# A sparse-attention and two-MLP kernel: weights loaded and converted in tiles of 512 columns with buffers of their own

## The chip, the cores and the metric

The kernel runs on one core of a Trainium2 chip. The metric is device time in microseconds (us), the median of several executions. TensorE does the matmuls, VectorE (DVE) and ScalarE (ACT) the elementwise work, SyncE (SP) issues the loads and stores.

## The reference

Attention with 4 batches, 8 heads, 576 positions and head size 64 is followed by two MLPs on 2304 tokens (512 to 2048 to 512). Half of the heads see the last 32 positions, the other half every 32nd position. All of it is float32, and the weights reach the kernel as float64.

```
scores = where(mask, scale * q @ k.T, -1e9);  attn = softmax(scores);  x = attn @ v
h = x @ w_in;   x = (s * relu(h)**2 + b) @ w_out          # first MLP
h = x @ w_in2;  out = (h * cos(h)) @ w_out2               # second MLP
```

## The kernel before

**Number format.** Every matmul of the MLPs is done three times on numbers that are split in a high and a low part: high x high, high x low, low x high. A weight tile is 128 x 512 numbers; `w` holds its high part and its low part. A weight arrives as a float64, so as two 32-bit words, and has to be put together as a float32 first. `convert_ops` does that on VectorE with four bit operations (L128 a multiplication, L129 a shift, L131 and L136 each a two-operand operation), into a tile `wtmp`. `split_hi` (L109, on ScalarE) then writes the high part and `split_lo` (L112, on VectorE) the low part.

**Where raw weights stand.** The pool `st` has four buffers of 2 KB a partition. A tile is loaded in two halves of 256 columns (`w_job`, L193 and L194, two `wraw`), and `wtmp` takes a third buffer of the same four. So a tile needs three of the four buffers, and the second half of the next tile waits for the first half of this one. The first four tiles, (0,0), (1,0), (0,1) and (1,1), are loaded whole at the start into space of the weights themselves (`w_early_load`, L155, `wearly`), and each of their operations has 512 columns. Key (n, k) is chunk n of the hidden dimension (0 to 15 first MLP, 16 to 31 second) and k the matrix (0 in, 1 out). 64 tiles are converted, 60 of them through `wraw`.

**Order.** The program is written as one sequence. MLP work goes in slots: 2 MLPs x 4 passes x 5 token blocks x 4 chunks = 160 slots. A slot has four groups of matmuls for `h` (`mm_h`, L521) and, for the slot two before it, four groups into the accumulators (`mm_2`, L575 and L578). After each group the program takes a step of attention (while there is any), of the elementwise stages, and of the background list `bg`: `bg_step(n)` adds n to a counter and issues one operation of a conversion for each whole one in it. n is BG0 = 1.5 in the first four slots, BG = 0.6 after that, and EARLY_BG = 0.6 for each step before them, when attention's first batch runs. `weight(n, k)` issues what is left of a conversion at once when a matmul needs it. In each pass of 20 slots the seven entries of `W_AT`, and one more line at its start, put the conversions of eight tiles on the list. A scheduling layer then moves instructions: on each engine they stand in the order that it chose.

**Attention around it.** A step of attention's softmax on VectorE is a maximum (L318), a scaling (L319), and, after ScalarE's exponentials, a sum step (L356), a reciprocal (L357) and the normalisation (L358), which TensorE's transposes (L366) wait for. The second MLP's elementwise chain ends with a multiplication on VectorE (L552) that reads `h_ps` and so frees its PSUM bank for the matmuls two slots later.

**Loads.** All DMAs are issued by SyncE, in its order: attention's `qk`, `v`, `rq`, `rs`, `rv`, then `wraw`, at the end `out`.

Of the kernel before, what the change touches and what calls it, by code (L numbers as in the profile page):

```python
# [8 lines left out]
F32 = mybir.dt.float32  # L9
F32R = mybir.dt.float32r  # L10
BF16 = mybir.dt.bfloat16
U32 = mybir.dt.uint32
AF = mybir.ActivationFunctionType
ALU = mybir.AluOpType
# [5 lines left out]
P = 128  # L20
NC = DM // P
NF = DFF // P
# [17 lines left out]
NWB = (7, 6)  # L40
W_AT = {3: (0, 0), 6: (0, 1), 9: (1, 0), 12: (1, 1), 15: (2, 0), 18: (3, 0), 19: (2, 1)}
W_AT0 = {8: (0, 0), 10: (0, 1), 12: (1, 0), 14: (1, 1), 15: (2, 0), 18: (3, 0), 19: (2, 1)}
BG = 0.6
BG0 = 1.5
RATE = [1.0, 0.6]
EARLY_BG = 0.6
ALAG = 3
NPB = 6
FIRST = [
# [32 lines left out]
def net(ctx, tc, qk, vloc, vstr, w1, w2, s, b, out):  # L82
    nc = tc.nc
    w_raw = [w1.bitcast(U32), w2.bitcast(U32)]
# [4 lines left out]
    st_p = ctx.enter_context(tc.tile_pool(name="st", bufs=4))  # L89
# [18 lines left out]
    def split_hi(dst_hi, src):  # L108
        nc.scalar.activation(dst_hi, src, AF.Copy)  # L109

    def split_lo(dst_lo, src, hi):
        nc.vector.tensor_tensor(dst_lo, src, hi.bitcast(F32), ALU.subtract)  # L112


    wtile, ready = {}, set()

    def convert_ops(raws, dst, key):

        tmp = st_p.tile([P, 512], F32, tag="st", name="wtmp")
        ops = []  # L120
        o = 0
        for raw in raws:
            n = raw.shape[1]
            t = tmp[:, o : o + n]
            tu = t.bitcast(U32)
            lo32, hi32 = raw[:, :, 0], raw[:, :, 1]
            o += n
            ops.append(lambda t=t, h=hi32: nc.vector.tensor_scalar(t, h.bitcast(F32), 2.0**-112, None, ALU.mult))  # L128
            ops.append(lambda tu=tu: nc.vector.tensor_scalar(tu, tu, 3, None, ALU.logical_shift_left))  # L129
            ops.append(  # L130
                lambda tu=tu, l=lo32: nc.vector.scalar_tensor_tensor(  # L131
                    tu, l, 29, tu, ALU.logical_shift_right, ALU.bitwise_or
                )
            )
            ops.append(
                lambda tu=tu, h=hi32: nc.vector.scalar_tensor_tensor(  # L136
                    tu, h, 0x80000000, tu, ALU.bitwise_and, ALU.bitwise_or
                )
            )
        ops.append(lambda: split_hi(dst[:, 0, :], tmp))  # L140
        ops.append(lambda: split_lo(dst[:, 1, :], tmp, dst[:, 0, :]))
        ops.append(lambda: ready.add(key))
        return ops

    def w_src(n, k, c0, c1):
        return w_raw[n // NF][n % NF, :, k, 2 * c0 : 2 * c1].rearrange("p (c t) -> p c t", t=2)

    def w_alloc(n, k):
        t = wp.tile([P, 2, 512], F32R, tag=f"w{k}", name=f"w{k}", bufs=NWB[k])
        wtile[n, k] = t  # L150
        return t

    def w_early_load(n, k):
        raw = wp.tile([P, 512, 2], U32, tag=f"w{k}", name="wearly", bufs=NWB[k])
        nc.sync.dma_start(out=raw, in_=w_src(n, k, 0, 512))  # L155
        return raw

    bg = []
# [3 lines left out]
    def bg_step(n):  # L162

        bg_due[0] = min(bg_due[0] + n, 4.0)
        while bg_due[0] >= 1 and (bg_now or bg):
            if not bg_now:
                bg_now.extend(bg.pop(0)())
            bg_now.pop(0)()
            bg_due[0] -= 1
# [13 lines left out]
    def tick():  # L183

        for g in list(stages):
            if next(g, "end") == "end":
                stages.remove(g)

    def w_job(n, k):

        raws = []
        for c in range(2):
            raw = st_p.tile([P, 256, 2], U32, tag="st", name="wraw")  # L193
            nc.sync.dma_start(out=raw, in_=w_src(n, k, 256 * c, 256 * (c + 1)))  # L194
            raws.append(raw)
        return convert_ops(raws, w_alloc(n, k), (n, k))


    qk_t, v_t, rem_t = {}, {}, {}
# [409 lines left out]
    for g in range(2):  # L609
        m = mloc[g * LG : (g + 1) * LG]  # L610
        for base, km, cm in ((-1, 1, -1), (32, -1, 1)):
            nc.gpsimd.affine_select(
                out=m, in_=m, compare_op=ALU.is_ge, fill=NEG, base=base, pattern=[[0, 4], [km, LK]], channel_multiplier=cm
# [3 lines left out]
    for base, pattern, cm in ((0, [[-NJ, 7], [-1, NJ]], 1), (NJ - 1, [[NJ, 7], [0, NJ]], -1)):  # L617
        nc.gpsimd.affine_select(
            out=mstr, in_=mstr, compare_op=ALU.is_ge, fill=NEG, base=base, pattern=pattern, channel_multiplier=cm
# [10 lines left out]
    raws = {}  # L630
    for what, *arg in FIRST:
        if what == "w":
            raws[tuple(arg)] = w_early_load(*arg)
        else:
            {"qk": load_qk, "v": load_v, "rq": load_rem_qk, "rv": load_rem_v}[what](0, *arg)
# [2 lines left out]

    for n, k in BG_ORDER:
        if n < 2:  # L640
            bg.append(lambda n=n, k=k: convert_ops([raws.pop((n, k))], w_alloc(n, k), (n, k)))
        else:
            bg.append(lambda n=n, k=k: w_job(n, k))
    att = Attention()
# [2 lines left out]
    while not att.batch_done(0):  # L647
        next(steps)
        tick()
        bg_step(EARLY_BG)  # L650
        if early < 2 and att.items[PRE + 2 * early].stored:
# [7 lines left out]
    def attention(n):  # L659
        if att.done:  # L660
            if acc_n[0] is None and not stages:
                acc_n[0] = 0
            return
        due[0] += n
        if due[0] >= 1:
            due[0] -= 1
            next(steps, None)

    for t in range(NSLOT + LAG):
        off = t % PER  # L670
        nxt = (t // PER + 1) * FP
        if nxt < 2 * NF:
            for o, (dn, k) in (W_AT if t >= PER else W_AT0).items():
                if off == o:
                    bg.append(lambda m=nxt + dn, k=k: w_job(m, k))
        if PER <= t < NSLOT and off == 0:
            bg.append(lambda m=nxt - FP + 3: w_job(m, 1))
        for blk, need in ((1, 1), (2, 2), (3, 3)):
            if t == blk * FP:
                while not att.batch_done(need):  # L680
                    next(steps, None)
                    tick()
        first = t < FP
        for c in range(8):
            if c < 4 and t < NSLOT and (t, c) not in ((0, 0), (0, 1)):
                mm_h(t, c)
            if c >= 4 and t >= LAG:
                mm_2(t - LAG, c - 4)
            tick()
            if c == 3 and t < NSLOT:  # L690
                spawn(run_act(t))
            attention(RATE[0] if first else RATE[1])
            bg_step(BG0 if first else BG)
    while stages:
# [56 lines left out]
```

## Time and profile before

| | us |
|---|---|
| median of 3 runs | 907.05 |
| lowest and highest | 906.38, 909.92 |
| the profiled execution | 908.91 |
| its span (first to last instruction) | 907.1 |
| TensorE busy | 898.8 (99%) |
| VectorE busy | 581.5 (64%) |
| ScalarE busy | 464.6 (51%) |
| mean granted TensorE clock | 0.985 |

The rows further down come from the profiled execution. An instruction's duration there runs from its start to its last write, and the next one on the same engine can start before that, so what one costs in a queue is the time from its start to the next start. "Idle before" with an arrow is the time in which the engine stood still and what ended it. A stage is a stretch of the span in us from its start.

### The profile page before, as it was taken

Reading aid. Unit: us, or ns where it says so; the run is one execution under the profiler, and the core shown is the slowest. Engines: PE = TensorE matmul, PEld = TensorE weight load, DVE = VectorE, ACT = ScalarE, POOL = GpSimd, SP = SyncE. Lnnn points to the kernel's source line nnn. Section 1 sums busy time; section 2 is a strip of 40 time slices with the busy share of each in tenths; the row PEclk is TensorE's granted clock in tenths of the full one; section 3 lists DMA queues with packets and bytes.
Section 4 is the critical chain, followed back from the end, with each engine's and each line's share of the span. In section 5 each row is a group of like instructions: output and inputs, shape, how many; then the busy total and the mean of one; then the engine's idle time right before and its main releaser. Section 6 shows DMA issues by size and latency. Waiting matters only on the chain.

```text
span 907.1 us, 12761 instructions
## 1 busy us (share of the span) xinstructions
PE 898.8 (99%) x4834; PEld 737.4 (81%) x4834; DVE 581.5 (64%) x1399; ACT 464.6 (51%) x1053; POOL 4.0 (0%) x15
## 2 busy tenths in 40 slices
PE   8999999999999999999999999999999999999998
PEld 5777777788888988888888888888888888888887
DVE  3488989448733784358645994479656984564444
ACT  3488876544433443344444755556445554454443
POOL 1000000000000000000000000000000000000000
PEclk8599999999999999999999999999999999999999
DMA  9345453002200230003100120013100220001111
GB/s 268 101 137 162 146 155 99 13 22 82 84 0 1 70 98 20 1 24 116 47 1 8 63 93 24 0 48 106 34 1 24 91 72 1 1 1 47 47 47 70
DMA packets 41486, 54.97 MB, mean 61 GB/s; under 512 B 7632, under 2 KB 21200, under 8 KB 41424
## 3 DMA queue, kind: packets, MB, share of 16 engines
q1 hardware_dynamic: 41424, 54.15, 18.7%
q8 instruction: 38, 0.62, 0.3%
q14 instruction: 24, 0.20, 0.1%
HBM read 49.42 MB, written 4.72 MB: 60 GB/s over the span
## 4 chain that ended last, share of the span: by engine, by line
PE 95%; DVE 2%; DMA 2%; SPq 0%; issue 0%
PE h_ps L521 43%; PE acc L578 22%; PE acc L575 21%; PE s_ps L300 4%; PE o_ps L398 3%; PE t_ps L366 2%; DMA wearly<-in_w_dram 1%; PE s_ps L296 0%; DMA wraw<-in_w_dram 0%; DVE part L592 0%; DVE xlo L112 0%; SPq L208 0%; DVE wtmp L131 0%; DVE wtmp L128 0%; DVE wtmp L136 0%; DVE part L358 0%
## 5 line engine op out<-in xcount | busy, mean ns | idle before, releaser
L521 PE MATMUL h_ps<-xhi,w 128*128 128x512 f32 (+1 forms) x1280 | 394.8, 371 | 0.8 <-DVE r L552 0.6
L521 PEld LDWEIGHTS h_ps<-xhi,w 128*128 128x128 f32 x1280 | 234.3, 189 | 43.7 <-DVE r L552 1.2
L521 PE MATMUL h_ps<-xlo,w 128*128 128x512 f32 (+1 forms) x640 | 236.3, 369 | 0.0
L575 PE MATMUL acc<-gh,w 128*128 128x512 f32 (+1 forms) x640 | 199.1, 372 | 0.0
L578 PE MATMUL acc<-w,gh 128*128 128x512 f32 x576 | 177.9, 390 | 0.0
L109 ACT ACTIVATE gh<-r 128x512 fp32r<-128x512 f32 (+1 forms) x160 | 94.1, 588 | 103.0 <-DVE r L552 52.6
L521 PEld LDWEIGHTS h_ps<-xlo,w 128*128 128x128 f32 x640 | 120.9, 189 | 19.7
L575 PEld LDWEIGHTS acc<-gh,w 128*128 128x128 f32 x640 | 117.0, 189 | 21.0 <-issue 0.7
L112 DVE TENSOR_TENSOR gl<-r,gh 128x512 fp32r<-128x512 f32 (+1 forms) x160 | 101.7, 635 | 48.1 <-ACT gh L109 46.9
L578 PEld LDWEIGHTS acc<-w,gh 128*128 128x128 f32 x576 | 107.1, 188 | 21.6 <-ACT gh L109 0.4
L575 PE MATMUL acc<-gl,w 128*128 128x512 f32 (+1 forms) x320 | 118.1, 369 | 0.0
L578 PE MATMUL acc<-w,gl 128*128 128x512 f32 x288 | 112.0, 389 | 0.0
L535 ACT ACTIVATE r<-h_ps 128x512 f32<-128x512 f32 (+1 forms) x80 | 44.1, 551 | 113.9 <-PE h_ps L521 113.7
L548 DVE SCALAR_TENSOR_TENSOR r<-a,r 128x512 f32<-128x512 f32 (+1 forms) x80 | 50.9, 636 | 65.8 <-ACT a L546 65.7
L592 DVE TENSOR_TENSOR part<-acc,part 128x512 f32<-128x512 f32 (+1 forms) x114 | 72.4, 657 | 30.1 <-PE acc L575 18.3
L541 DVE TENSOR_SCALAR r<-r,sb 128x512 f32<-128x512 f32 (+1 forms) x72 | 37.1, 515 | 78.1 <-ACT r L536 77.9
L550 ACT ACTIVATE r<-r 128x512 f32<-128x512 f32 (+1 forms) x80 | 47.2, 590 | 64.1 <-DVE r L548 64.0
L545 ACT ACTIVATE r<-h_ps 128x512 f32<-128x512 f32 (+1 forms) x80 | 44.2, 553 | 69.5 <-PE h_ps L521 68.8
L552 DVE TENSOR_TENSOR r<-h_ps,r 128x512 f32<-128x512 f32 (+1 forms) x80 | 50.8, 635 | 27.1 <-ACT r L550 26.8
L575 PEld LDWEIGHTS acc<-gl,w 128*128 128x128 f32 x320 | 60.4, 189 | 9.4
L578 PEld LDWEIGHTS acc<-w,gl 128*128 128x128 f32 x288 | 54.1, 188 | 11.5 <-DVE gl L112 0.2
L109 ACT ACTIVATE w<-wtmp 128x512 fp32r<-128x512 f32 x64 | 40.1, 626 | 23.5 <-DVE wtmp L136 21.3
(66 smaller groups left out, 780.5 us busy)
## 6 DMA issues: line engine op xcount, KB each, us to landing
wraw<-in_w_dram SPq DMA_DIRECT2D x120, 256.0 KB, 3.1
out_dram<-part SPq DMA_DIRECT2D x18, 256.0 KB, 2.0
qk<-in_qk_dram SPq DMA_DIRECT2D x8, 544.0 KB, 4.2
v<-in_vloc_dram SPq DMA_DIRECT2D x8, 384.0 KB, 3.8
qk<-in_qk_dram SPq DMA_DIRECT2D x6, 504.0 KB, 4.3
wearly<-in_w_dram SPq DMA_DIRECT2D x4, 512.0 KB
v<-in_vstr_dram SPq DMA_DIRECT2D x6, 252.0 KB
part<-in_qk_dram SPq DMA_DIRECT2D x2, 504.0 KB
```

Of the source, the lines that this page charges most:

```text
L109: nc.scalar.activation(dst_hi, src, AF.Copy)
L112: nc.vector.tensor_tensor(dst_lo, src, hi.bitcast(F32), ALU.subtract)
L521: nc.tensor.matmul(h_ps[t][:, :tb], wt[:, wi, c * P : (c + 1) * P], xt[:, c, t0 : t0 + tb], start=(c == 0 and i == 0), stop=(c == NC - 1 a ...
L535: nc.scalar.activation(r, h, AF.Relu)
L541: nc.vector.tensor_scalar(r, r, sb[:, 0:1], sb[:, 1:2], ALU.mult, ALU.add)
L545: nc.scalar.activation(r, h, AF.Copy, bias=0.25, scale=INV_2PI)
L548: nc.vector.scalar_tensor_tensor(r, a, MAGIC, r, ALU.subtract, ALU.subtract)
L550: nc.scalar.activation(r, r, AF.Sin, scale=-TWO_PI)
L552: nc.vector.tensor_tensor(r, h, r, ALU.mult)
L575: nc.tensor.matmul(o, wt[:, wi, e * P : (e + 1) * P], g, start=st, stop=sp, skip_group_check=True)
L578: nc.tensor.matmul(o, g[:, e * P : (e + 1) * P], wt[:, wi, :], start=st, stop=sp, skip_group_check=True)
L592: nc.vector.tensor_tensor(dst, o, dst, ALU.add)
```

## The change

A late weight tile is loaded in one DMA of 512 columns into a buffer `raw` of its own (two of 4 KB a partition). `wtmp` has two buffers (its tag `st` now asks for two), and is no longer shared with raw weights. Each of the four bit operations runs once over 512 columns. A late tile has 6 operations in the background list and had 11 (8 bit operations, two splits and an entry that only marks it done); an early one has 6 and had 7. The rates per step are cut from 0.6 to 0.36 and from 1.5 to 0.9. The region that the compiler keeps for descriptors of dynamic DMAs is set to 4096 bytes to make room.

```diff
-BG = 0.6
-BG0 = 1.5
+BG = 0.36
+BG0 = 0.9
 RATE = [1.0, 0.6]
-EARLY_BG = 0.6
+EARLY_BG = 0.36
...
-    def convert_ops(raws, dst, key):
+    def convert_ops(raw, dst, key):
-        tmp = st_p.tile([P, 512], F32, tag="st", name="wtmp")
-        for raw in raws:
-            n = raw.shape[1]
-            t = tmp[:, o : o + n]
...
+        t = st_p.tile([P, 512], F32, tag="st", name="wtmp", bufs=2)
+        tu = t.bitcast(U32)
+        lo32, hi32 = raw[:, :, 0], raw[:, :, 1]
+        return [
+            lambda: nc.vector.tensor_scalar(t, hi32.bitcast(F32), 2.0**-112, None, ALU.mult),
+            lambda: nc.vector.tensor_scalar(tu, tu, 3, None, ALU.logical_shift_left),
+            lambda: nc.vector.scalar_tensor_tensor(tu, lo32, 29, tu, ALU.logical_shift_right, ALU.bitwise_or),
+            lambda: nc.vector.scalar_tensor_tensor(tu, hi32, 0x80000000, tu, ALU.bitwise_and, ALU.bitwise_or),
+            lambda: split_hi(dst[:, 0, :], t),
+            lambda: (split_lo(dst[:, 1, :], t, dst[:, 0, :]), ready.add(key)),
+        ]
...
     def w_job(n, k):
-        raws = []
-        for c in range(2):
-            raw = st_p.tile([P, 256, 2], U32, tag="st", name="wraw")
-            nc.sync.dma_start(out=raw, in_=w_src(n, k, 256 * c, 256 * (c + 1)))
-            raws.append(raw)
-        return convert_ops(raws, w_alloc(n, k), (n, k))
+        raw = st_p.tile([P, 512, 2], U32, tag="raw", name="wraw", bufs=2)
+        nc.sync.dma_start(out=raw, in_=w_src(n, k))
+        return convert_ops(raw, w_alloc(n, k), (n, k))
...
-    nc = _bacc.Bacc("TRN2", target_bir_lowering=False, num_devices=1)
+    nc = _bacc.Bacc("TRN2", target_bir_lowering=False, num_devices=1, dynamic_dma_scratch_size=4096)
```

The file is 17 lines shorter, so L341 after is L358 before, and so on; in `convert_ops` L128, L129, L131 and L136 become L123 to L126.

**How it moves instructions.** First VectorE, in the last part of attention's first batch. `sm_496`, `sm_534` and `sm_567` are the softmax statistics of three consecutive items before; after, the same items are `sm_493`, `sm_531` and `sm_562`. Before:

```order
L318 TENSOR_REDUCE sm_567<-s_ps_557 128x4
L358 TENSOR_TENSOR part_89<-part_89,sm_496 128x384
L319 TENSOR_SCALAR sm_567<-sm_567 128x4
L131 SCALAR_TENSOR_TENSOR wtmp_555<-wearly_163,wtmp_555 128x512
L356 TENSOR_SCALAR sm_534<-sm_534 128x4
L128 TENSOR_SCALAR wtmp_676<-wearly_165 128x512
L357 RECIPROCAL sm_534<-sm_534 128x4
L136 SCALAR_TENSOR_TENSOR wtmp_555<-wearly_163,wtmp_555 128x512
L358 TENSOR_TENSOR part_89<-part_89,sm_534 128x384
```

The same place after:

```order
L341 TENSOR_TENSOR part_89<-part_89,sm_493 128x384
L339 TENSOR_SCALAR sm_531<-sm_531 128x4
L301 TENSOR_REDUCE sm_562<-s_ps_552 128x4
L340 RECIPROCAL sm_531<-sm_531 128x4
L125 SCALAR_TENSOR_TENSOR wtmp_625<-wearly_163,wtmp_625 128x512
L341 TENSOR_TENSOR part_89<-part_89,sm_531 128x384
```

The normalisation of the second item (L358, now L341) has one conversion between the maximum and itself, and had three.

Next SyncE, where the first raw weights are loaded through the new buffers. `wraw_734` and `wraw_736` are the two halves of one tile before, `wraw_871` and `wraw_893` two whole tiles after. Before:

```order
L219 DMA v_539<-in_vloc_dram 96x8x128
L208 DMA qk_537<-in_qk_dram 128x2x504
L237 DMA rv_615<-in_vloc_dram 96x128
L238 DMA rv_615<-in_vstr_dram 72x128
L237 DMA rv_615<-in_vloc_dram 96x128
L238 DMA rv_615<-in_vstr_dram 72x128
L194 DMA wraw_734<-in_w1_dram 128x512
L208 DMA qk_613<-in_qk_dram 128x2x504
L194 DMA wraw_736<-in_w1_dram 128x512
```

The same place after:

```order
L202 DMA v_536<-in_vloc_dram 96x8x128
L178 DMA wraw_871<-in_w1_dram 128x1024
L191 DMA qk_534<-in_qk_dram 128x2x504
L178 DMA wraw_893<-in_w1_dram 128x1024
L220 DMA rv_609<-in_vloc_dram 96x128
L191 DMA qk_607<-in_qk_dram 128x2x504
L221 DMA rv_609<-in_vstr_dram 72x128
```

Two whole weight tiles stand ahead of the `rv` loads and of one `qk` load behind which half a tile stood.

Last VectorE at the start of the second MLP. `w0_5127` before and `w0_4866` after are the same weight tile, and `r_4936` and `r_4731` the first slot's product with the cosine, which frees the PSUM bank of `h_ps`. Before:

```order
L112 TENSOR_TENSOR w0_5127<-wtmp_5128,w0_5127 128x512
L548 SCALAR_TENSOR_TENSOR r_4936<-a_4937,r_4936 128x512
L128 TENSOR_SCALAR wtmp_5230<-wraw_5225 128x256
L128 TENSOR_SCALAR wtmp_5230<-wraw_5227 128x256
L129 TENSOR_SCALAR wtmp_5230<-wtmp_5230 128x256 x2
L131 SCALAR_TENSOR_TENSOR wtmp_5230<-wraw_5225,wtmp_5230 128x256
L131 SCALAR_TENSOR_TENSOR wtmp_5230<-wraw_5227,wtmp_5230 128x256
L136 SCALAR_TENSOR_TENSOR wtmp_5230<-wraw_5225,wtmp_5230 128x256
L136 SCALAR_TENSOR_TENSOR wtmp_5230<-wraw_5227,wtmp_5230 128x256
L552 TENSOR_TENSOR r_4936<-h_ps_4921,r_4936 128x512
```

The same place after:

```order
L126 SCALAR_TENSOR_TENSOR wtmp_4867<-wraw_4864,wtmp_4867 128x512
L123 TENSOR_SCALAR wtmp_4981<-wraw_4978 128x512
L124 TENSOR_SCALAR wtmp_4981<-wtmp_4981 128x512
L112 TENSOR_TENSOR w0_4866<-wtmp_4867,w0_4866 128x512
L125 SCALAR_TENSOR_TENSOR wtmp_4981<-wraw_4978,wtmp_4981 128x512
L531 SCALAR_TENSOR_TENSOR r_4731<-a_4732,r_4731 128x512
L126 SCALAR_TENSOR_TENSOR wtmp_4981<-wraw_4978,wtmp_4981 128x512
L123 TENSOR_SCALAR wtmp_5105<-wraw_5102 128x512
L124 TENSOR_SCALAR wtmp_5105<-wtmp_5105 128x512
L125 SCALAR_TENSOR_TENSOR wtmp_5105<-wraw_5102,wtmp_5105 128x512
L535 TENSOR_TENSOR r_4731<-h_ps_4717,r_4731 128x512
```

The next tile's conversion is started before the first product and most of a third one stands ahead of it as well; `wraw_5102` uses the buffer of `wraw_4864`.

## Rows read from the trace of the kernel before

**Rows 1.** The page: busy us (share of span) x instructions of each engine.

```profile
PE 898.8 (99%) x4834; PEld 737.4 (81%) x4834; DVE 581.5 (64%) x1399; ACT 464.6 (51%) x1053; POOL 4.0 (0%) x15
```

**Rows 2.** Stages: us; busy PE, PEld, DVE, ACT, POOL; clock; DMA share, GB/s.

```profile
0.00:17.00 17.00, 13.70 (x102) 7.45 (x103) 5.87 (x18) 5.69 (x27) 4.02 (x15) 1.00 0.93 264
17.00:44.00 27.00, 27.00 (x158) 18.92 (x156) 13.69 (x49) 12.77 (x54) 0.00 (x0) 0.50 0.48 143
...
50.90:54.50 3.60, 2.74 (x39) 1.86 (x39) 3.57 (x13) 3.60 (x22) 0.00 (x0) 1.00 0.56 182
54.50:180.50 126.00, 126.00 (x1012) 95.90 (x1013) 103.08 (x338) 94.27 (x322) 0.00 (x0) 1.00 0.40 123
...
498.00:520.00 22.00, 21.44 (x128) 19.01 (x127) 19.96 (x48) 16.03 (x31) 0.00 (x0) 1.00 0.22 73
...
880.00:907.10 27.10, 23.55 (x125) 19.68 (x123) 12.55 (x24) 10.31 (x22) 0.00 (x0) 1.00 0.15 59
```

**Rows 3.** Chain of waits, in both MLPs: start us, us, what.

```profile
240.16 2.72 PE h_ps L521 x12
...
640.83 2.72 PE h_ps L521 x12
```

**Rows 4.** Order of time, VectorE, 504 to 515 us: start us, us, instruction.

```profile
504.46 0.69 DVE L112 TENSOR_TENSOR w<-wtmp,w 128x512 fp32r<-128x512 f32 x1
...
505.99 0.29 DVE L128 TENSOR_SCALAR wtmp<-wraw 128x256 f32<-128x256 f32 x1
506.19 0.42 DVE L131 SCALAR_TENSOR_TENSOR wtmp<-wraw,wtmp 128x256 uint32<-128x256 uint32 x1
506.52 0.42 DVE L112 TENSOR_TENSOR gl<-r,gh 128x256 fp32r<-128x256 f32 x1
...
512.21 0.29 DVE L128 TENSOR_SCALAR wtmp<-wraw 128x256 f32<-128x256 f32 x1 [0.79 <-DMA wraw<-in_w_dram]
...
514.17 0.68 DVE L552 TENSOR_TENSOR r<-h_ps,r 128x512 f32<-128x512 f32 x1
```

**Rows 5.** Order of time, VectorE, 51.9 to 53 us.

```profile
51.94 0.69 DVE L131 SCALAR_TENSOR_TENSOR wtmp<-wearly,wtmp 128x512 uint32<-128x512 uint32 x1
52.54 0.16 DVE L356 TENSOR_SCALAR sm<-sm 128x4 f32<-128x4 f32 x1
52.61 0.42 DVE L128 TENSOR_SCALAR wtmp<-wearly 128x512 f32<-128x512 f32 x1
52.95 0.17 DVE L357 RECIPROCAL sm<-sm 128x4 f32<-128x4 f32 x1
```

**Rows 6.** Groups by form, VectorE: count | busy us, mean ns | idle before.

```profile
L131 DVE SCALAR_TENSOR_TENSOR wtmp<-wraw,wtmp 128x256 uint32<-128x256 uint32 x120 | 50.2, 420 | 0.9
```

**Rows 7.** Order of time, VectorE and TensorE, around 15 us.

```profile
14.67 0.43 DVE L128 TENSOR_SCALAR wtmp<-wearly 128x512 f32<-128x512 f32 x1 [1.84 <-DMA wearly<-in_w_dram]
...
16.82 0.88 PE L366 MATMUL t_ps<-ident,part 128*96 128x128 f32 x4 [1.71 <-DVE part L358]
```

**Rows 8.** Order of time, TensorE, 52 to 59 us.

```profile
52.10 0.61 PE L366 MATMUL t_ps<-ident,part 128*96 128x128 f32 x4 [0.57 <-DVE sm L319]
...
53.89 0.50 PE L521 MATMUL h_ps<-xhi,w 128*128 128x512 f32 x1 [0.21 <-ACT xhi L109]
54.47 0.64 PE L366 MATMUL t_ps<-ident,part 128*96 128x128 f32 x4
...
58.77 0.64 PE L366 MATMUL t_ps<-ident,part 128*96 128x128 f32 x4
```

**Rows 9.** Order of time, TensorE, at 515 us.

```profile
514.91 0.50 PE L521 MATMUL h_ps<-xhi,w 128*128 128x512 f32 x1 [0.56 <-DVE r L552]
```

**Rows 10.** The page, DMA issues: count, KB each, median us to landing.

```profile
wraw<-in_w_dram SPq DMA_DIRECT2D x120, 256.0 KB, 3.1
...
qk<-in_qk_dram SPq DMA_DIRECT2D x6, 504.0 KB, 4.3
```

**Rows 11.** Waits: who for whom, us in total, times, longest us.

```profile
DVE wtmp L128 <- DMA wraw<-in_w_dram: 14.3, 21, 1.8
```

More of the change, by code (lines that the diff above doesn't have):

```diff
@@ L115, in net, with w_src @@
     wtile, ready = {}, set()
-    def convert_ops(raws, dst, key):
-        tmp = st_p.tile([P, 512], F32, tag="st", name="wtmp")
-        ops = []
-        o = 0
-        for raw in raws:
-            n = raw.shape[1]
-            t = tmp[:, o : o + n]
[L125 to L146, printed above, removed]
+    def convert_ops(raw, dst, key):
[10 more added lines that the diff above has]
+        ]
+    def w_src(n, k):
+        return w_raw[n // NF][n % NF, :, k, :].rearrange("p (c t) -> p c t", t=2)
     def w_alloc(n, k):
@@ L154, in w_early_load @@
         raw = wp.tile([P, 512, 2], U32, tag=f"w{k}", name="wearly", bufs=NWB[k])
-        nc.sync.dma_start(out=raw, in_=w_src(n, k, 0, 512))
+        nc.sync.dma_start(out=raw, in_=w_src(n, k))
         return raw
@@ L189, in w_job @@
     def w_job(n, k):
-        raws = []
-        for c in range(2):
-            raw = st_p.tile([P, 256, 2], U32, tag="st", name="wraw")
-            nc.sync.dma_start(out=raw, in_=w_src(n, k, 256 * c, 256 * (c + 1)))
-            raws.append(raw)
-        return convert_ops(raws, w_alloc(n, k), (n, k))
+        raw = st_p.tile([P, 512, 2], U32, tag="raw", name="wraw", bufs=2)
+        nc.sync.dma_start(out=raw, in_=w_src(n, k))
+        return convert_ops(raw, w_alloc(n, k), (n, k))
     qk_t, v_t, rem_t = {}, {}, {}
@@ L640, in net @@
         if n < 2:
-            bg.append(lambda n=n, k=k: convert_ops([raws.pop((n, k))], w_alloc(n, k), (n, k)))
+            bg.append(lambda n=n, k=k: convert_ops(raws.pop((n, k)), w_alloc(n, k), (n, k)))
         else:
```

## The prediction

> **What bounds the kernel now.** I read the page's table of engines first, then the granted clock and busy time by stage, then the chain of waits, and only then the lines that the diff touches. TensorE is busy 898.8 of the 907.1 us [rows 1]. "Busy" alone could mislead, since pipelined matmuls overlap in the record, so the second view cuts the span into stages [rows 2]: TensorE is idle for 3.30 us before 17 us, 0.86 us in 50.9 to 54.5, 0.56 us in 498 to 520 and 3.55 us in the tail after 880. That is 8.3 us, all that rows 1 leave, so there is no gap anywhere else: not in the half-clock stretch and not in the crowded 54.5 to 180.5. From 17 to 44 us the granted clock is 0.50 (1.2 GHz), in the other stages shown 1.00 (2.4 GHz); that stretch costs at most half of its 27 us, 13.5 us. The chain of waits shows the same: twelve full matmuls take 2.72 us while VectorE is lightly loaded (240 us) and 2.72 us while it carries its heaviest mix (641 us) [rows 3], so VectorE does not slow a matmul down, it can only delay its start.
>
> VectorE is 64% busy over the span, but 103.1 of 126.0 us in 54.5 to 180.5, where attention, MLP and conversions overlap, and 20.0 of 22.0 us at the change of MLP in 498 to 520 [rows 2]. The diff takes work from VectorE and SyncE only, so it can give back no more than those TensorE gaps that VectorE or a weight load ends, and it can cost whatever new gaps VectorE makes.
>
> The Trainium skill, Perfetto Trace Analysis, Identifying the Most-Contended Engine, warns that matmul busy share is a poor measure of TensorE's headroom and that the busy share of weight loads is better. That share is 81% here [rows 1], which read that way would leave 170 us. The equal 2.72 us of rows 3 says that no part of it is reachable by freeing VectorE, so I go by the gaps.
>
> **The change part by part.**
>
> *Fewer, wider conversion instructions.* Each of the 60 weight tiles that are loaded late now has four bit operations of 512 columns instead of eight of 256. From start to next start, on a queue that does not wait, a 256-column multiply or shift takes 0.20 us and a 256-column two-operand operation 0.33 us (starts at 505.99, 506.19, 506.52) [rows 4]; with 512 columns these are 0.34 us (52.61 to 52.95) and 0.60 us (51.94 to 52.54) [rows 5]. Per tile: 4 x 0.20 + 4 x 0.33 = 2.12 us before, 2 x 0.34 + 2 x 0.60 = 1.88 us after, so 0.24 us less, and 60 x 0.24 = 14.4 us of VectorE in all. (Sixty tiles: 120 instructions of each 256-column form [rows 6].) None of it is on the path, except in the two gaps below. It is covered by TensorE's own work in the stages without a gap.
>
> *Pacing.* One step of the background counter was 0.6 of 11 operations (18.3 steps a tile; 7 operations, 11.7 steps, for the four early tiles) and is 0.36 of 6 (16.7 steps). Late tiles come a little sooner and early tiles later. The wish to have tiles (1,0), (2,0) and (3,0) in time decides at slots 1 to 3; the order on VectorE has the last conversion of these at nearly the same place among attention's instructions as before. I cost it at 0.
>
> *The start, 0 to 44 us.* TensorE's longest stall, 1.71 us at 15.1, is the chain from the first early weight load: VectorE's first conversion waits 1.84 us for it, the normalisation stands behind it, and the transposes wait for that [rows 7]. The clock falls right behind this stall. The order on VectorE is the same in both kernels up to the fourth conversion of that tile, and SyncE issues the same loads in the same order up to there. So the stall stays, and the half-clock stretch starts where it did: 0. When the clock rises again I can only bound. It rose at about 44 us, while the first 512-column matmuls of the MLP ran, and those stand a few instructions elsewhere in TensorE's new order, between other small matmuls. The nearest measure for what such a shift is worth are the three runs of before, the same program each time: they lie 3.5 us apart. I take half of that either way, -1.8 to +1.8 us, value 0.
>
> *50.9 to 54.5 us.* TensorE waits 0.57 us before the transposes at 52.10 and 0.21 us before the matmul at 53.89, and the transposes at 54.47 wait for a normalisation on VectorE [rows 8]. In front of that normalisation VectorE had three conversions (0.60, 0.34 and again 0.60 us, by rows 5). In the new order one stands there; two come behind it. The next item's normalisation gets three in front, but its transposes come at 58.77, 4.3 us after the late ones at 54.47 [rows 8], which covers them. Gain 0.4 us; bounds 0.9 (all idle gone) and -0.9 (as much again).
>
> *498 to 520 us.* Here a load is late. VectorE waits 0.79 us for it, converts, and only then multiplies (514.17), which frees the PSUM bank that the matmul at 514.91 needs, 0.56 us late [rows 4, 9]. The new order still ends in a late load: three tiles are converted in a row, and the third needs the first one's buffer. Adding the steps in the new order from the subtraction at 504.46 [rows 4]: 0.60 + 0.34 + 0.33 + 0.34 + 0.60 + 0.33 + 0.60 + 0.60 = 3.7 us (a subtraction of 512 columns taken like a two-operand conversion), so the buffer is free at 508.2. A load twice as large as the 3.1 us one is nearest to the 504 KB row, 4.3 us [rows 10]: 512.5. Then 0.34 + 0.34 + 0.60 us, and the multiply starts at 513.8, not 514.17. Gain 0.3 us; bounds 0.56 and -0.6 (the load queues behind another for 1 us).
>
> *Loads.* 60 of 512 KB replace 120 of 256 KB. With two buffers of their own, the first two are issued ahead of the query and key loads that they stood behind. VectorE waited for such loads 21 times, 14.3 us in all [rows 11]; most of that goes, behind TensorE's work. What is queued behind a new wait on VectorE is a step of MLP or attention; outside the two gaps TensorE did not wait for any of them. The query and key loads that are moved back by one weight load (at most 4.3 us) are for the next batch and wait for buffers freed by TensorE. Cost 0, bounds 0 and +1. All issues in the trace are SyncE's, none of VectorE or GpSimd, so nothing reads the descriptors' region that shrinks: 0, both bounds.
>
> *The sum.* -0.4 - 0.3 = -0.7 us on a span of 907.1, whose execution took 908.91 us. The median of the runs, 907.05, is 1.86 us below that one. So 907.05 - 0.7 = 906.4 us.
>
> **The rivals.**
>
> *Coarser steps hold TensorE up (slower).* A two-operand conversion now blocks VectorE 0.60 us at a stretch, not 0.33. 60 x 2 of them could each add 0.27 us, 32 us if each one ended a TensorE wait. For it: VectorE is 82% busy in 54.5 to 180.5, and the multiply that frees the bank in the second MLP has been late once already. Against it: the waits of TensorE that end with VectorE, in 907 us, are 1.71, 0.57 and 0.56 us [rows 7 to 9]. It decides from 17 of the 120 on the path: 907.05 + 17 x 0.27 = 911.6; I would put it at 912. The Trainium skill, Perfetto Trace Analysis, Optimizing Scalar/DVE Operations, says the same as a rule: where VectorE is not saturated but makes bubbles on other engines, breaking instructions up may let work finish sooner, and this change does the reverse. By rows 2 the bubbles are 1.4 us.
>
> *A second fall of the clock (slower).* If the new order leaves TensorE as idle around 52 us as it was at 15 to 17 us, the clock falls again, and a second stretch like 17 to 44 costs 13.5 us: 920.5. For it: 0.86 of 3.60 us are idle there now and the clock held. Against it: fewer conversions stand in that place.
>
> *An earlier rise (faster).* 4.5 us less needs the rise 9 us sooner, at 35 us, before the first 512-column matmul: 902.5.
>
> *The change moves nothing.* The scheduler fills VectorE as before, a late load ends the same two gaps: 907.1.
>
> **How the numbers follow.** Forecast 0.72, nothing moves 0.12 (both within 0.5%, 4.5 us, about what a measurement can tell from no change), coarser steps 0.07, second fall 0.05, earlier rise 0.04. So same 0.84, slower 0.12, faster 0.04. The range takes in the bounds: 906.4 - 1.8 - 0.7 = 903.9 below; above, 906.4 + 1.8 + 0.9 + 0.6 + 1.0 = 910.7. I give 904.0 to 910.7.
>
> **What would show it.** Right: TensorE's stall near 15 us and the fall of the clock behind it unchanged; VectorE 10 to 20 us less busy; few waits for weight loads; no new TensorE gap over 0.6 us. Wrong: a rise of the clock far from 44 us, a second stretch at 0.50, or gaps that VectorE's conversions end between 54 and 180 us or wherever three tiles are converted in a row.

## The result

| | median of all runs, us | range | runs | ratio to before |
| --- | --- | --- | --- | --- |
| before, same session | 908.92 | 906.38 to 909.92 | 6 | |
| changed | 916.47 | 912.24 to 921.01 | 6 | 1.0082 [1.0053, 1.0111] |
| before, later session | 909.15 | 905.94 to 911.23 | 26 | |
| changed, same program again | 912.81 | 910.48 to 918.79 | 9 | 1.0049 [1.0027, 1.0071] |

The forecast was 906.4 us, range 904.0 to 910.7, with 0.84 on no change. The changed kernel is slower, by 3.7 us in one session and 7.5 in the other, and its runs lie between 910 and 921 us. (Ratios leave out runs over 1.5% above the fastest of their kernel, which are one of `h2` and two of `h3` below; medians and ranges hold all.)

The page after, in the place of [rows 1], and the waits that answer to [rows 7, 11]:

```profile
PE 903.5 (99%) x4834; PEld 740.8 (81%) x4834; DVE 562.6 (61%) x1159; ACT 466.8 (51%) x1053; POOL 4.0 (0%) x15
```

```profile
PE t_ps L349 <- DVE part L341: 6.3, 2, 5.2
...
DVE wtmp L123 <- DMA wearly<-in_w_dram: 5.4, 1, 5.4
...
DVE wtmp L123 <- DMA wraw<-in_w_dram: 3.5, 5, 2.2
```

VectorE lost 18.9 us of work and its waits for late weights fell from 14.3 us to 3.5. Yet TensorE, with the same 4,834 matmuls, is busy 4.7 us longer. A busy time that grows with the same work points to the clock, and the stages show it (us; busy PE, PEld, DVE, ACT, POOL; clock; DMA share, GB/s; to be read against [rows 2]):

```profile
17.00:20.20 3.20, 0.00 (x0) 0.00 (x0) 2.13 (x9) 0.43 (x2) 0.00 (x0) 0.50 0.41 112
20.20:51.00 30.80, 30.78 (x167) 21.22 (x167) 15.06 (x54) 14.53 (x61) 0.00 (x0) 0.50 0.45 143
51.00:56.60 5.60, 5.60 (x69) 3.94 (x68) 3.27 (x14) 3.69 (x16) 0.00 (x0) 1.00 0.05 5
56.60:57.70 1.10, 0.03 (x1) 0.03 (x1) 1.00 (x3) 1.10 (x9) 0.00 (x0) 1.00 0.79 236
57.70:64.40 6.70, 6.70 (x44) 4.64 (x44) 4.93 (x17) 4.20 (x19) 0.00 (x0) 0.51 0.47 163
...
507.50:529.50 22.00, 22.00 (x132) 19.62 (x132) 21.46 (x44) 16.16 (x32) 0.00 (x0) 1.00 0.23 72
```

Three things differ from before. The wait in the head is longer and the first half-clock stretch ends at 51, not 44 us. At 56.6 us TensorE is idle for a whole microsecond, where it had waited 0.57, and **behind that gap the clock falls a second time**, to 64.4 us. The gap at 515 us [rows 9] is gone: the change of MLP comes some 9.5 us later here, and TensorE is busy in all of 507.5 to 529.5 us. The wait in the head:

```profile
20.22 1.09 PE L349 MATMUL t_ps<-ident,part 128*96 128x128 f32 x4 [5.22 <-DVE part L341]
```

What half clock costs is in TensorE's rows right around that place. From their start to the next start, the same 16 score products take 0.80 us at full clock (55.50 to 56.30) and 1.47 us at half (60.19 to 61.66):

```profile
55.50 0.88 PE L283 MATMUL s_ps<-qk 64*64 64x96 f32 x16
56.30 0.33 PE L381 MATMUL o_ps<-part,rv 96*64 96x64 f32 x2
57.70 0.33 PE L349 MATMUL t_ps<-ident,part 128*96 128x128 f32 x1 [1.07 <-DVE part L341]
57.96 1.17 PE L381 MATMUL o_ps<-part,rv 96*64 96x64 f32 x14
59.06 0.88 PE L349 MATMUL t_ps<-ident,part 128*96 128x128 f32 x3
59.73 0.53 PE L279 MATMUL s_ps<-mloc,identb 128*128 128x384 bf16 x1
60.19 1.55 PE L283 MATMUL s_ps<-qk 64*64 64x96 f32 x16
61.66 1.09 PE L349 MATMUL t_ps<-ident,part 128*96 128x128 f32 x4
```

So a busy microsecond at half clock loses 1 - 0.80/1.47 = 0.46 us; taking these products for all is an estimate. The account of this run, whose span is 8.8 us longer: head wait +3.5 (5.22 for 1.71); first stretch 30.8 busy us for about 27.4 (to 44.4 us), 3.4 x 0.46 = +1.6; second stretch 6.7 x 0.46 = +3.1; gap at 57 us +0.3 (1.07 for 0.57 + 0.21); a new gap at 145 us +0.6; the gap at 515 us -0.6. That is 8.5 of 8.8.

The rows above also show why TensorE stood still. The transposes at 57.70 belong to item 10, the first of attention's second batch, and wait for its normalisation. Behind the first of them in the queue stand 14 records, seven of the eight value products (57.96), that were ready. In the kernel before all eight stand ahead of the transposes that [rows 8] show at 52.10:

```profile
50.82 0.70 PE L398 MATMUL o_ps<-part,rv 96*64 96x64 f32 x16
```

VectorE at that time, in the changed kernel:

```profile
55.07 0.56 DVE L301 TENSOR_REDUCE sm<-s_ps 128x4 f32<-128x384 f32 x1 [1.51 <-PE s_ps L283]
55.54 0.42 DVE L123 TENSOR_SCALAR wtmp<-wearly 128x512 f32<-128x512 f32 x1
55.87 0.16 DVE L339 TENSOR_SCALAR sm<-sm 128x4 f32<-128x4 f32 x1
55.95 0.16 DVE L302 TENSOR_SCALAR sm<-sm 128x4 f32<-128x4 f32 x1
56.02 0.42 DVE L124 TENSOR_SCALAR wtmp<-wtmp 128x512 uint32<-128x512 uint32 x1
56.35 0.17 DVE L340 RECIPROCAL sm<-sm 128x4 f32<-128x4 f32 x1
56.44 0.65 DVE L112 TENSOR_TENSOR xlo<-o_ps,xhi 128x504 fp32r<-128x504 f32 x1
57.01 0.55 DVE L341 TENSOR_TENSOR part<-part,sm 128x384 f32<-128x384 f32 x1
```

VectorE first waits for the next item's scores (55.07), and between that maximum and the normalisation (57.01) stand two conversion steps, 0.33 us each from start to next start, and a subtraction.

### The profile page after: what moved, and what is told of

Its sections match the earlier page's. It is cut to its first block, busy times and chain, and to the rows that moved or that the text cites. A ratio compares the mean times of both kernels' runs of the same rounds, so it can differ in the third digit from the quotient of the medians.

```text
span 915.9 us, 12379 instructions
## 1 busy us (share of the span) xinstructions
PE 903.5 (99%) x4834; PEld 740.8 (81%) x4834; DVE 562.6 (61%) x1159; ACT 466.8 (51%) x1053; POOL 4.0 (0%) x15
## 4 chain that ended last, share of the span: by engine, by line
PE 95%; DMA 2%; DVE 1%; SPq 1%; ACT 0%; issue 0%; ACTq 0%
PE h_ps L504 43%; PE acc L561 21%; PE acc L558 21%; PE s_ps L283 4%; PE o_ps L381 3%; PE t_ps L349 2%; DMA wearly<-in_w_dram 1%; DMA wraw<-in_w_dram 1%; PE s_ps L279 0%; SPq L202 0%; SPq L191 0%; DVE part L341 0%; DVE wtmp L125 0%; DVE part L575 0%; ACT part L326 0%; DVE wtmp L123 0%
## 5 line engine op out<-in xcount | busy, mean ns | idle before, releaser
L528 ACT ACTIVATE r<-h_ps 128x512 f32<-128x512 f32 (+1 forms) x80 | 44.4, 555 | 72.8 <-PE h_ps L504 72.3
L112 DVE TENSOR_TENSOR w<-wtmp,w 128x512 fp32r<-128x512 f32 x64 | 43.9, 686 | 9.1 <-ACT w L109 8.4
```

The lines of the kernel that those rows point to most:

```text
L528: nc.scalar.activation(r, h, AF.Copy, bias=0.25, scale=INV_2PI)
```

## The experiments

Twelve kernels ran in three sessions, each beside the kernel before (909.31, 909.15 and 909.0 us).

**First session: the region, the rates, the load's place.** The long wait in the head suggested the smaller descriptors' region, since SyncE's issues are slower from the fifth load on: the first weight tile is issued at 5.96 us, not 4.62.

`e1`, the kernel before with the small region alone:

```
-    nc = _bacc.Bacc("TRN2", target_bir_lowering=False, num_devices=1)
+    nc = _bacc.Bacc("TRN2", target_bir_lowering=False, num_devices=1, dynamic_dma_scratch_size=4096)
```

> The kernel before with one change: the descriptors' region is cut from 16,384 to 4,096 bytes per partition; tiles, buffers and rates stay. Theory A (the smaller region slows the issue of the first loads): the first weight tile is issued at about 6.0 us and lands at about 18 us, as in the changed kernel (before 4.62 and 14.64), TensorE's wait in the head is about 5 us instead of 1.71, its half-clock stretch ends near 48 to 51 us instead of 44.4, and the time is 911 to 917 us. Theory B (the new tiles and rates do it; the region is free, as the prediction has it): the tile lands at 14.6 us, the wait stays 1.7 us, and the time is 906 to 910 us. Theory C (the head's loads merely vary from run to run): landing anywhere between, time within 0.3% of the kernel before.

Measured: 908.35 us (906.39 to 910.69, 12 runs), ratio 0.9996 [0.9982, 1.0009].

```profile
17.65 1.09 PE L366 MATMUL t_ps<-ident,part 128*96 128x128 f32 x4 [3.41 <-DVE part L358]
...
53.43 0.61 PE L366 MATMUL t_ps<-ident,part 128*96 128x128 f32 x4 [0.57 <-DVE sm L319]
```

The first weight tile is issued at 6.01 us, as theory A has it, and the head's wait was 3.41 us, but the time is that of before. Theory A falls on the time; nor does the region alone set the issue, which is at 4.63 us in e3 below with the same 4,096 bytes. It is also visible that the wait of 1.71 us, which the prediction took as fixed, is one draw: the queues are the same up to there, and the profiled runs of kernels with the early conversion show 1.71 to 5.22.

`e2`, the changed kernel with a region of 12,288 bytes:

```
-    nc = _bacc.Bacc("TRN2", target_bir_lowering=False, num_devices=1, dynamic_dma_scratch_size=4096)
+    nc = _bacc.Bacc("TRN2", target_bir_lowering=False, num_devices=1, dynamic_dma_scratch_size=12288)
```

> The changed kernel with its descriptors' region at 12,288 bytes instead of 4,096 (its buffers need 4 KB more than the old ones and no more); all else as changed. Theory A (region): the first weight tile lands near 14.6 us again, the wait in the head is near 1.7 us, the clock is back near 44 us and the time is 904 to 910 us. Theory B (tiles and rates): the landing stays near 18 us or the second fall of the clock near 57 us stays, and the time is 913 to 918 us.

Measured: 911.82 us (903.99 to 916.09, 12 runs), ratio 1.0041 [1.0017, 1.0065]: still slower, with the changed kernel's spread. Its profiled run has the same gap of 1.07 us, and the clock held behind it:

```profile
53.10:54.20 1.10, 0.03 (x1) 0.07 (x1) 1.00 (x4) 1.10 (x9) 0.00 (x0) 1.00 0.89 324
54.20:66.00 11.80, 11.80 (x114) 9.09 (x115) 11.63 (x34) 10.31 (x40) 0.00 (x0) 1.00 0.46 138
```

So the gap is a property of the program (1.07 us in both profiled runs of this order so far), and the fall behind it comes in a part of the runs.

`e3`, the changed kernel with the old rates (`BG = 0.6`, `BG0 = 1.5`, `EARLY_BG = 0.6`):

> The changed kernel with the old rates of conversions per step (0.6, 1.5 and 0.6 instead of 0.36, 0.9 and 0.36); tiles and region as changed. Theory A (region): the landing near 18 us and the long wait in the head stay, time 912 to 917 us; at most the 1.07 us gap at 56.6 us and the second half-clock stretch behind it (6.5 us, worth about 3.2 us) move. Theory B (the order that the rates make): gap and second stretch go, and the wait in the head with them, 906 to 909 us.

Measured: 911.61 us (908.38 to 915.41, 12 runs), ratio 1.003 [1.0014, 1.0046]. Neither theory: the order is a third one. TensorE waits 0.99 us at 51 us, this time for ScalarE's evacuation, then 0.49 us, and the clock is at half from there to 58.7 us.

```profile
52.10 0.74 PE L381 MATMUL o_ps<-part,rv 72*64 72x72 f32 x6 [0.99 <-ACT part L357]
53.33 0.79 PE L504 MATMUL h_ps<-xhi,w 128*128 128x512 f32 x1 [0.49 <-ACT xhi L109]
```

`e4`, the changed kernel with the first weight load ahead of two loads of v:

```
+    ("w", 0, 0),
     ("v", 0),
     ("v", 1),
-    ("w", 0, 0),
```

> The changed kernel with the first weight tile's load put ahead of the first two loads of v (region, tiles and rates as changed). Theory A (issue slowed by the region from the fifth load on, and VectorE blocked behind the conversion of this tile): the tile is issued near 3.4 us and lands near 14 us, VectorE's wait for it falls from 5.4 to under 2 us, TensorE's wait from 5.2 to under 2 us, the half-clock stretch ends some 3 to 6 us sooner, time 908 to 913 us. Theory B (tiles and rates): the head's wait shrinks too, but the second fall near 57 us stays, time 912 to 916 us. If v, now later, is waited for instead, TensorE's wait only moves to the first products with v.

Measured: 913.73 us (906.44 to 914.74, 12 runs), ratio 1.0043 [1.0023, 1.0062]. The tile was there at 11.5 us, but the scheduler had set its first conversion ahead of the first maxima, so VectorE stood for it from the start; TensorE waited 4.09 us at 11.6 us, for ScalarE's exponentials, and 1.51 us at 47 us, with a stretch at half clock to 60 us behind that. The head's wait only moved.

**Second session: fill the gap.** By now the theory (D) was that the time follows from TensorE's idle time and the half-clock stretches, and that the gap at item 10 sets off the second one.

`f1`, the changed kernel again:

> The changed kernel itself a second time, beside the next three on one chip. Theory D (what the four runs so far leave): the time is the start of the first scores, plus TensorE's idle time, plus what its half clock loses, plus a constant 878 us of work at full clock (it was 877.8 to 878.3 in six profiled runs). In every run of the changed kernel TensorE waits 1.07 us near 53 to 58 us for VectorE's normalisation of item 10, and in a part of the runs the clock falls to half behind it for 6 to 7 us (3 to 3.5 us lost); the head's wait varies from run to run (1.7 to 5.2 us) with the landing of the first weight tile. So: gap of 1.07 us again, head's wait anywhere in that span, runs spread over 907 to 918 us, some with and some without the second fall. Theory E (the first profile is typical): landing near 18 us and wait of 5 us again, 914 to 918 us in the median.

Measured: 912.81 us (910.48 to 918.79, 9 runs). The head's wait was 2.35 us, the gap 1.07 again, and the clock fell behind it:

```profile
54.77 0.42 PE L349 MATMUL t_ps<-ident,part 128*96 128x128 f32 x1 [1.07 <-DVE part L341]
```

```profile
48.50:54.20 5.70, 5.19 (x66) 3.57 (x60) 3.81 (x15) 4.03 (x19) 0.00 (x0) 1.00 0.10 19
54.20:55.30 1.10, 0.54 (x5) 0.34 (x7) 1.00 (x4) 0.81 (x6) 0.00 (x0) 0.72 1.04 389
55.30:61.80 6.50, 6.50 (x44) 4.62 (x44) 4.39 (x16) 4.18 (x19) 0.00 (x0) 0.52 0.44 146
```

The nine runs fall into six with a mean granted clock of 0.979 or less (median 913.96 us) and three above (910.76), 3.2 us apart, about what a second stretch costs. The profiled runs of this program with the fall lie in the first group (0.977, 0.979), e2's without it in the second (0.983).

`h2` and `h3`, dummy products into the transposes' bank ahead of item 10's transposes, two and three of them:

```
 WARM = 18
+FILL = {(1, 0, 0): 3}
...
         def transp(self, tag):
             self.t_ps = psum(tag, "t_ps")
+            for _ in range(FILL.get((self.bb, self.hp, self.j), 0)):
+                nc.tensor.matmul(
+                    self.t_ps[:, : 4 * LK],
+                    identb,
+                    mloc.rearrange("p n k -> p (n k)"),
...
```

> The changed kernel with two dummy matrix products (128 x 384 columns, bf16, about 0.16 us each at full clock) into the transposes' bank ahead of item 10's transposes, which in TensorE's queue still stand ahead of seven of the eight value products of items 8 and 9. Theory D: the gap shrinks from 1.07 to about 0.75 us, the second fall becomes rarer or not, 908 to 916 us; it is the control for the next run. Rival (the gap has nothing to do with the fall): as the changed kernel run beside it, within 1 us.

> The same with three dummy products. With the third one the scheduler sets item 10's transposes behind the seven value products (about 1.2 us of work that was ready), and nothing else of the order moves. Theory D: TensorE has work in the whole wait, the gap near 53 to 58 us is under 0.2 us, no second fall of the clock, and the median falls by 1 us (the gap) plus 2 to 3.3 us (the fall, in the part of runs that had it) against the two kernels beside it: 905 to 911 us. Rival (the fall comes from the rate of work after the low stretch, not from the gap): a fall near 57 us stays, 911 to 916 us.

Measured: 911.51 us (908.39 to 922.5, 12 runs), ratio 1.0025 [1.0013, 1.0038], and 910.03 us (903.36 to 918.62, 12 runs), ratio 1.0009 [0.9991, 1.0027]. TensorE in h3, and the stages behind it:

```profile
53.10 0.66 PE L347 MATMUL t_ps<-mloc,identb 128*128 128x384 bf16 x3 [0.52 <-DVE xlo L113]
53.78 0.70 PE L391 MATMUL o_ps<-part,rv 96*64 96x64 f32 x14
54.41 0.64 PE L359 MATMUL t_ps<-ident,part 128*96 128x128 f32 x4
```

```profile
52.00:54.00 2.00, 1.47 (x19) 0.76 (x17) 1.90 (x7) 1.72 (x10) 0.00 (x0) 1.00 0.74 223
54.00:66.00 12.00, 12.00 (x117) 9.12 (x113) 11.83 (x35) 10.55 (x39) 0.00 (x0) 1.00 0.44 139
```

The gap did not go below 0.2 us, against what theory D expected, because the dummies wait 0.52 us themselves for the subtraction that frees the bank; it is 0.52 us in both kernels, about the 0.57 us of before. Neither profiled run shows the second fall. With the gap cut in two and all else as changed, h3's median is 0.9 us above the kernel before, which its ratio cannot tell from no change, although its head wait was 3.34 us and two of its runs took about 918 us. h2 is no control, since two dummies already halve the gap; it still is 2.4 us above before, which the counts below explain in part.

`g4`, h3 and a gate: the first conversion waits for item 1's normalisation, so VectorE does not stand in the head for the weight tile:

```
+        if key == (0, 0):
+            nc.scalar.activation(t[:, 0:1], att.items[1].sm[:, 2, 0:1], AF.Copy)
...
-    bg_due = [0.0]
+    bg_due = [-3.0]
```

> The kernel with three dummy products, and in addition the first conversion waits for item 1's normalisation (ScalarE writes one column of the conversion's tile from it), so that VectorE does not stand in the head for the first weight tile's landing. Theory D: VectorE's wait for the weight tile (1.8 to 5.4 us so far) and with it TensorE's wait in the head go below 1 us, the runs spread less, and the time falls by 1 to 4 us against the kernel without it: 901 to 908 us, less if the clock no longer falls at 17 us (its loss is 13.4 us). Rival (the head's wait is ruled by the first exponentials and not by the weight tile): the wait stays above 1.5 us and the time as without it. Since conversions come later, a wait for the first weights near 40 us would show as a gap there.

Measured: 902.54 us (897.29 to 904.85, 6 runs), ratio 0.9927 [0.9903, 0.9952]. The head's wait is gone; the clock falls all the same, at 24 us and without a gap ahead of it, for 14 us instead of 27 to 34 in the profiled runs without the gate (17 in e4). A new gap of 0.87 us (ScalarE's evacuation for the value products) has a stretch at a low clock behind it:

```profile
12.70:24.00 11.30, 11.30 (x105) 8.73 (x105) 8.23 (x28) 10.29 (x53) 0.00 (x0) 1.00 0.93 263
24.00:38.00 14.00, 14.00 (x96) 10.32 (x94) 9.57 (x34) 5.77 (x23) 0.00 (x0) 0.51 0.72 200
...
43.40:44.40 1.00, 0.13 (x3) 0.01 (x2) 1.00 (x4) 1.00 (x9) 0.00 (x0) 1.00 1.08 413
44.40:52.00 7.60, 7.60 (x49) 5.61 (x50) 5.28 (x19) 4.95 (x24) 0.00 (x0) 0.55 0.44 148
```

**Third session: the one number, and a better kernel.** The order of instructions says which part of the diff moves item 10: `EARLY_BG`, tried alone in the kernel before. (In the changed kernel only all three rates were put back, in e3.) TensorE in the kernel before with 0.36 in it (`o_ps<-part,rv` are the value products):

```
L398 MATMUL o_ps<-part,rv 64x64
L366 MATMUL t_ps<-ident,part 96x128
L398 MATMUL o_ps<-part,rv 64x64 x3
L398 MATMUL o_ps<-part,rv 64x72 x4
L366 MATMUL t_ps<-ident,part 96x128 x3
```

With 0.6 all eight value products stand ahead of the four transposes. `j1` is that kernel:

```
-EARLY_BG = 0.6
+EARLY_BG = 0.36
```

> The kernel before with one number changed: the rate of conversions per step of the first attention batch is 0.36 instead of 0.6; its tiles, buffers, region and later rates stay. The scheduler then sets the first of item 10's four transposes ahead of seven value products, as in the changed kernel. Theory D (that order is the cause): TensorE's gap of about 1.07 us near 53 to 57 us and, in most runs, the second half-clock stretch behind it appear in the old kernel too: 910.5 to 916 us. Rival (the gap matters only with the new tiles and buffers): 906 to 910 us, as the kernel before.

Measured: 910.82 us (907.74 to 919.82, 12 runs), ratio 1.0045 [1.0017, 1.0072].

```profile
55.37 0.28 PE L366 MATMUL t_ps<-ident,part 128*96 128x128 f32 x1 [1.07 <-DVE part L358]
```

```profile
49.50:54.20 4.70, 4.70 (x58) 3.29 (x58) 3.19 (x14) 2.97 (x14) 0.00 (x0) 1.00 0.04 4
54.20:55.40 1.20, 0.13 (x3) 0.06 (x1) 1.10 (x3) 1.20 (x10) 0.00 (x0) 1.00 0.83 254
55.40:63.00 7.60, 7.60 (x50) 5.60 (x51) 4.90 (x17) 5.01 (x24) 0.00 (x0) 0.55 0.42 132
```

The old tiles, buffers and region, with one number changed, have the same gap to the hundredth, a second stretch of nearly the same length and two groups of runs (five with a median of 914.31 us, seven of 909.79).

Counting runs by the mean granted clock: with the gap of 1.07 us, 0.979 or less in 21 of 39 runs (5 of 6, 6 of 9, e2 5 of 12, j1 5 of 12); with a gap of 0.52 or 0.57 us, none of 78 runs of before, none of 12 of e1, 3 of 24 of h2 and h3. The mean is a sign of the second stretch and no view of it: the profiled runs of e3 and e4 have one at 0.981 and 0.985, because their first stretch ended early (41.7 and 29.5 us).

The same counts show a second difference, apart from item 10's gap. Of the 90 runs of before and e1, 36 have a mean clock of 0.985 to 0.987; the 30 of before among them have a median of 907.1 us, its 47 at 0.981 to 0.984 one of 909.8. Of the 63 runs of the changed kernel, e2, h2, h3 and j1, none lies at 0.985 to 0.987 (two lie above, at 903.4 and 904.0 us). By the clock in rows of 1 us, the first stretch at half clock lasts about 27 us in before's profiled run (0.985), 31 in e1's (0.982), and 31 to 34 in the profiled runs of those five. So with `EARLY_BG` at 0.36 the shorter runs of before are missing as well, by some 2.7 us each, and a filled gap does not bring them back; what makes the first stretch longer is not shown.

`j2` and `j3`, the gate in the kernel before and in the changed one, no dummies:

> The kernel before, with its first conversion made to wait for item 1's normalisation (one column of the conversion's tile is written by ScalarE from it), as in the run with the gate above. Theory D: VectorE no longer stands for the first weight tile, TensorE's wait of 1.7 to 3.4 us in the head goes, the clock falls later and stays low for less; 900 to 906 us. Rival (the gate pays only with the new tiles): 906 to 910 us.

> The changed kernel with the same gate and no dummy products. Theory D: as the old kernel with the gate, within 2 us of it (it keeps 0.6 us from the gap at 514 us that went, and loses as much to a gap near 130 to 145 us): 900 to 906 us. If the tiles of 512 columns cost something beyond the two places in the first 60 us, it is above the old kernel with the gate by 3 us or more.

Measured: 902.09 us (899.13 to 905.22, 6 runs), ratio 0.9925 [0.9902, 0.9948], and 904.14 us (898.51 to 905.91, 6 runs), ratio 0.9937 [0.9912, 0.9962]. The two cannot be told apart (2 us between medians of six runs each), so the tiles of 512 columns cost and gain nothing that six runs show, once the head is out of the way. In both profiled runs the clock holds far beyond 24 us. In j2's it falls behind three waits of 0.36 to 0.49 us within 2.6 us:

```profile
36.70:39.30 2.60, 1.27 (x19) 0.91 (x18) 2.52 (x11) 1.99 (x13) 0.00 (x0) 1.00 0.55 187
39.30:52.50 13.20, 11.98 (x77) 9.01 (x77) 8.89 (x30) 8.22 (x38) 0.00 (x0) 0.50 0.34 94
```

In j3's it holds behind a wait of 1.79 us and falls behind one of 1.36 us:

```profile
28.98 0.38 PE L285 MATMUL s_ps<-qk 64*64 64x96 f32 x2 [1.79 <-DMA qk<-in_qk_dram]
...
40.45 0.70 PE L383 MATMUL o_ps<-part,rv 96*64 96x64 f32 x14 [1.36 <-ACT part L359]
```

```profile
29.00:38.80 9.80, 9.61 (x101) 7.00 (x102) 6.97 (x28) 5.75 (x25) 0.00 (x0) 1.00 0.69 148
...
41.30:48.00 6.70, 6.70 (x34) 4.76 (x33) 4.31 (x13) 4.55 (x22) 0.00 (x0) 0.50 0.38 114
```

So the length of a wait alone does not decide whether the clock falls.

`j4`, g4 with six dummy products ahead of the value products of items 8 and 9:

```
         o = psum(tag, "o_ps")
+        for _ in range(6 if it.kind == "rem" and it.bb == 0 else 0):
+            nc.tensor.matmul(
+                o[:, : 4 * LK], identb, mloc.rearrange("p n k -> p (n k)"), start=True, stop=True, skip_group_check=True
+            )
```

> The changed kernel with the gate, three dummy products ahead of item 10's transposes and six ahead of the value products of items 8 and 9, which waited 0.87 us for ScalarE at 43.5 us in the run with the gate above. Theory D: that gap is filled, the second half-clock stretch behind it (7 us long, 2.2 us lost) goes, and the time falls by 1.5 to 3 us against the run with the gate above: 898 to 902 us, the lowest of all. Rival (the clock falls again anyway): 901 to 905 us, with a stretch at half clock that begins at 44 us without a gap.

Measured: 898.25 us (894.5 to 904.82, 6 runs), ratio 0.989 [0.9858, 0.9922], faster than both kernels. Its interval overlaps g4's, so what the six dummies add to the gate is not shown. In its profiled run, the fastest of the six, the clock never falls:

```profile
8.00:24.00 16.00, 15.59 (x181) 11.82 (x179) 11.67 (x38) 13.30 (x63) 0.00 (x0) 1.00 0.90 260
24.00:45.00 21.00, 19.99 (x208) 13.82 (x206) 18.49 (x66) 16.26 (x72) 0.00 (x0) 1.00 0.72 217
45.00:66.00 21.00, 21.00 (x201) 16.35 (x199) 18.71 (x56) 18.49 (x63) 0.00 (x0) 1.00 0.52 156
```

## Where the prediction was right and wrong

- **Conversions, -14.4 us on VectorE, none of it on the path.** Right: -18.9 us busy, and TensorE's full matmuls did not get shorter. In the trace after, a 512-column two-operand conversion takes 0.60 us to the next start where nothing waits (519.38 to 519.98), as costed.
- **Loads and the descriptors' region, 0.** Right: waits for late weights fell to 3.5 us, and the region alone measured 0.9996.
- **498 to 520 us, gain 0.3.** Right in sign, 0.56 us measured, its upper bound. The load that was to end this place late is not late: the third tile's conversion starts 7.3 us behind the subtraction (513.99 to 521.30) where 8.0 was forecast, and VectorE waits for no weight there. A gap of 0.63 us at 145 us that was not there before, behind a mask addition on VectorE (that engine's longest wait for a late weight, 2.2 us, lies just ahead of it), takes it back.
- **50.9 to 54.5 us, gain 0.4. This step failed.** The prediction followed VectorE's order and one item, the second of the three shown there (item 11): its normalisation does have one conversion ahead of it instead of three. The item ahead of it, 10, got two conversions and a subtraction between a wait and its normalisation, just above the rows shown; before, none stood there (50.93 to 51.41). And TensorE's own new order was not looked at: there item 10's first transpose had moved ahead of seven ready value products. A slip of VectorE that those products would have covered for the most part (0.70 us at full clock, in h3) became a gap of 1.07 us.
- **Pacing, 0. The source of that step's error.** The rates were read as "Late tiles come a little sooner and early tiles later", with the weights still in time. No TensorE wait for a weight contradicts that, but the scheduler lays out TensorE's queue anew for it, and not only VectorE's. `EARLY_BG` alone gives the gap, the second fall and a ratio of 1.0045 in the old kernel.
- **The second fall of the clock, 0.05 at 920.5 us.** The mechanism was named, with its place; the argument against it ("fewer conversions stand in that place") was the failed step again, and the gap that sets it off was put at that of the head (1.71 us), while 1.07 us was enough in three of four profiled runs. Its price was too high: the stretch was taken as long as the first (13.5 us), and in these runs it is 6.5 to 7.6 us long and costs about 3.
- **The start, 0, bounds 1.8 either way. This term was mis-sized.** The order was as said, but the stall was not a constant 1.71 us: in the profiled run the longer wait (+3.5) and the longer first stretch (+1.6) are more than half of the 8.8 us, and the clock rose at 51 us, not 44. e1 and j1 show that a wait of 3.4 to 3.9 us there comes without the new tiles as well, so that part is no effect of the change that is shown. In every profiled run that has the stall the clock falls in it or right behind it, but it is not the only cause: with the stall removed the clock held beyond 38 us in j2, j3 and j4 and fell at 24 us in g4 without one. What stays open: in the first session the median lay 7.5 us above before, of which the gap and the fall (in five of six runs) explain about 3.5. The profiled run of it had 3.5 us more wait in the head; whether the other five had it too is not recorded.
- **The base and the range.** 907.05 us was a median of three runs; six in the same session give 908.92 and the later ones 909.0 to 909.3, so 2 us of the miss lay in the base, by the luck of which runs were at hand. And the upper end adds losses of 0.9 and 0.6 us, counted from no change, to a forecast that already holds gains of 0.4 and 0.3: it should be 911.4, not 910.7. The first session's 916.47 us lies above both.
- **Coarser steps.** Little sign of it: one wait of TensorE, the 0.63 us at 145 us, has wide conversions just ahead on VectorE, and with the gap filled the changed kernel's median is 0.9 us above the old one.

## What to carry to other kernels

Where a scheduler lays out the queues, a pacing number is an edit of every engine's order: compare the order of the engine that bounds, not only of the one whose work changes, and look for an instruction that waits ahead of ready work. While TensorE's clock is in play, price a gap by what follows it: here 0.5 us more idle cost 3 us in about half of the runs. Runs that fall into groups by granted clock can point to such a place, but not alone, since those of before do so too; a few dummy products in the place put it to the test.

## What the runs showed of the hardware that was not expected

- A gap of TensorE of 1.07 us, soon after the clock had risen, was followed by a fall to half clock in three of four profiled runs and not in the fourth; gaps of 0.52 to 0.57 us at the same place in none of four (before, e1, h2, h3). The Trainium skill, TensorE: Matmul & The Clock Gate, Why this matters for your kernels, warns of idle gaps in mid-kernel, though of longer ones than this; the trace agrees in kind, and for the length the measurement decides. Length is not all: in j3 the clock held behind a wait of 1.79 us and fell behind one of 1.36.
- The clock fell without a gap as well, at 24 us in g4 after 11.3 us of uninterrupted work, and did not in j2, j3 and j4 with the same gate. What set that off the runs do not say.
- Cutting the descriptors' region to a quarter changed nothing measurable with all loads issued by SyncE: 0.9996 [0.9982, 1.0009].
